# A fixed instruction order from a table, shared gate and up weights, and earlier closing waits in a fused attention and ReGLU kernel

## The chip, the core and the metric

The kernel runs on one core of a Trainium2 chip. The core has five engines that run side by side, each through its own list of instructions in order: PE (TensorE, matmuls, with PEld for its weight loads), ACT (ScalarE), DVE (VectorE), POOL (GpSimd) and SP (SyncE, which here only issues DMA transfers). They meet only through semaphores: an instruction can wait for a semaphore to reach a value, and can raise one when it is done. The metric is the time of one execution in microseconds (us) of device time, lower being better, as the median over runs.

## What is computed

The inputs are `x` of 2048 rows and 512 columns in bfloat16, and weights. The result is the input plus attention plus a gated feed-forward network, both on the same normalised input:

```python
xn  = layernorm(x)                                  # per row, eps 1e-5
qkv = xn @ wqkv                                     # 512 -> 3 * 512, 32 heads of 16
p   = softmax(q @ k.T / 4)                          # 32 heads, 2048 x 2048 scores each
att = (p @ v) @ wo
gate, up = xn @ W_gate, xn @ W_up                   # 512 -> 1792
ffn = (gate * (gate > 0) * up) @ W_down
out = x + att + ffn
```

The 32 x 2048 x 2048 = 134 million exponentials of the softmax are the peculiar part: heads are only 16 wide, so there is little matmul work for each exponential.

## The kernel before

**Tiles.** The 2048 query rows are cut into four blocks (`c4`), the 32 heads into four groups of eight (`gg`) and each group into its even and odd heads (`ee`): 32 blocks of four heads by 512 queries. Within a block the kernel goes through 16 tiles of 128 keys (`kt`). Scores stand in PSUM with keys on the partitions and 512 queries along the row, one head to a bank.

**Two ways to an exponential.** For most key tiles two *units* are made, each with two heads: two score matmul groups fill two PSUM banks, and one ACT instruction (line 1419) takes the exponential of 128 x 1024 values into a buffer `ring` of 16 places. There are 720 units; two pairs of banks are used in turn, so the scores of unit u wait until the exp of unit u-2 has read its banks. For the other key tiles, 152 in all and called *quads* (function `quad`), the exponential is approximated without ACT: DVE turns each head's scores into 16-bit integers that are the bit patterns of a power of two (`d1`, line 1372, 608 of them), and two shifted copies of these patterns are made, on POOL (line 1388, in two pieces each) or on DVE (line 1392). PE sums all three patterns.

**Matmuls.** Nearly all matmuls are of one form, issued by a helper at line 122: 64 x 32 weights with 512 moving columns. Four of them side by side make a *group*, and a group uses the lower or the upper half of the array's rows; groups on the two halves run at the same time. The weights of a group are loaded by four separate instructions (lines 1352 for scores, 1324 for values, 846 for the rest), and these are left out where the half still holds the same weights. Behind each unit and quad come groups that multiply the exponentials by the values (`pv_stream`) and add up in PSUM; a column of ones beside the values gives the sums of the softmax.

**The rest of the work** is laid between the units: projections of q, k and v (`proj_q`, `proj_k`, `proj_v`), the feed-forward network (`glu` makes 128 of the 1792 hidden columns for one block of 512 rows; `out_rows` multiplies by `W_down` and `wo` and stores the result), and the division by the sums (`normalise`), which goes through transfers of the sums to DRAM and back. A projected q is spread over `qT` by eight transfers of 16 KB. `glu` streams its gate and up weights from DRAM for two neighbouring hidden tiles at once, in two transfers of 128 KB each, into one of two buffers; it does so anew for every block of rows, which makes 56 transfers for each of the two. Four banks of PSUM are shared by all this, by the quads' scores and by the sums of `pv_stream`.

**The order.** All operations are first recorded in a graph (`Graph.op`) with an assumed duration, a priority, and what they read and write. `Graph.run` then places them one after the other: each time it takes the operation that could start first by the assumed durations, among those close together the one with the better priority, and gives it a buffer (`slot_for`, `ready`, `pick_pe`). What it leaves is a fixed list for each engine. `Graph.emit` works out which semaphore waits are needed, and `play` writes the instructions. On PE a load for the other half may be put ahead of a waiting group. The lists of the chip are thus static; an engine that waits holds up all that stands behind it in its own list.

**The end.** After the last unit `normalise_last` brings in the last block on a shorter path: a copy on ACT (line 1190), sums and transposes on DVE, eight more groups on PE, three additions on DVE and one copy on ACT, and four stores (line 1221). Each transfer belongs to a stream, and each stream has a semaphore; there are 102. At the very end SP waits for all of them (line 550):

```python
            if e == "SP":
                for s, v in fin:
                    eng.wait_ge(s, v)
```

## Time and profile before

| what | value |
|---|---|
| time, median of three runs | 695.08 us (691.43, 695.08, 696.24) |
| span of the profiled execution, the only time given of it | 696.8 us |
| PE busy | 678.8 us, 97% |
| PEld busy | 385.5 us, 55% |
| ACT busy | 671.8 us, 96% |
| DVE busy | 603.4 us, 87% |
| POOL busy | 504.2 us, 72% |
| DMA | 40.65 MB, mean 58 GB/s |

The page of the profile gives, for each engine, the busy time and its share, and for groups of equal instructions their count, their busy time together, the mean duration of one in ns, and the idle time of the engine just before them with what ended it. A group's busy time is shorter than count times mean where instructions overlap, as exps and matmuls do. "Issue" stands for time in which an engine waited for nothing that the profile shows. The chain is followed back from the last instruction, each time to what released it. Ends of matmuls are modelled, so that a busy PE is not PE at its peak. The mean clock granted to PE was 0.999 of full speed.

### The profile page before, as it was taken

What the parts mean: (1) busy time and instruction counts of PE and PEld (TensorE: products, weight loads), DVE (VectorE), ACT (ScalarE), POOL (GpSimd) and SP (SyncE); (2) the same over time, 40 slices, a digit from 0 to 9 for tenths busy, and PEclk for the clock granted to TensorE, in tenths of its full rate; (3) what the DMA queues carried; (4) which work ended last, traced back from release to release, by engine and by line L of the source; (5) the groups of instructions that cost most, each with busy time, mean ns of one, the idle gap of its engine ahead of it and who ended that gap; (6) DMA issues with size and microseconds to landing.
All of it is one profiled execution on the core that took longest, in us unless ns stands there. A gap on an engine that the chain in (4) does not pass through costs nothing.

```text
span 696.8 us, 46210 instructions
## 1 busy us (share of the span) xinstructions
PE 678.8 (97%) x22229; PEld 385.5 (55%) x20884; DVE 603.4 (87%) x1009; ACT 671.8 (96%) x733; POOL 504.2 (72%) x511
## 2 busy tenths in 40 slices
PE   8999999999999999999999999999999999999996
PEld 4556565555654656455655455654655575655663
DVE  9958899999899688888999887899999788899875
ACT  6999999999999999999999999999999999999994
POOL 3323759767689786868979787787778886786871
PEclk9999999999999999999999999999999999999999
DMA  7330312153201121211211121122210121221001
GB/s 212 71 65 6 92 46 63 46 140 96 63 27 40 41 80 55 52 47 56 68 35 33 41 78 49 49 62 58 58 54 25 48 72 50 62 58 40 27 17 48
DMA packets 65736, 40.65 MB, mean 58 GB/s; under 512 B 19912, under 2 KB 61576, under 8 KB 65544
## 3 DMA queue, kind: packets, MB, share of 16 engines
q1 hardware_dynamic: 65544, 37.69, 19.8%
q8 instruction: 169, 2.77, 1.7%
q14 instruction: 23, 0.19, 0.1%
HBM read 31.06 MB, written 2.35 MB: 48 GB/s over the span
## 4 chain that ended last, share of the span: by engine, by line
PE 62%; ACT 33%; DVE 2%; issue 1%; SPq 0%; DMA 0%; DVEq 0%
PE ps L122 61%; ACT ring L1419 32%; DVE qd L1372 1%; PE ps L950 1%; SPq L1288 0%; DVE xn_sb L775 0%; DVE v_aug L911 0%; DMA x_sb<-oT 0%; PE ps L800 0%; ACT qT L993 0%; PE ps L1434 0%; PE ps L968 0%; ACT xnT L808 0%; PE ps L1175 0%; DVEq L552 0%
## 5 line engine op out<-in xcount | busy, mean ns | idle before, releaser
L1419 ACT ACTIVATE ring<-ps 128x1024 bf16<-128x1024 f32 x720 | 665.5, 1102 | 8.5 <-PE ps L122 7.3
L1388 POOL TENSOR_TENSOR qd<-qd,ints 128x512 int32<-128x512 int32 x450 | 454.7, 1042 | 148.8 <-DVE qd L1392 58.7
L122 PE MATMUL ps<-qT,kT 64*32 64x512 bf16 x8192 | 463.5, 375 | 4.1 <-issue 0.9
L1372 DVE TENSOR_SCALAR qd<-ps 128x512 int16<-128x512 f32 x608 | 395.6, 684 | 56.5 <-PE ps L122 51.5
L122 PE MATMUL ps<-qd,v_aug 64*32 64x512 bf16 x3648 | 294.1, 375 | 1.3 <-issue 1.2
L122 PE MATMUL ps<-ring,v_aug 64*32 64x512 bf16 x2880 | 249.9, 375 | 0.5
L1352 PEld LDWEIGHTS <-kT 64*32 64x32 bf16 x7972 | 171.8, 92 | 123.8 <-issue 35.6
L1324 PEld LDWEIGHTS <-v_aug 64*32 64x32 bf16 x5400 | 131.8, 92 | 73.7 <-issue 18.6
L122 PE MATMUL ps<-xnT,wus 64*32 64x512 bf16 x1792 | 138.3, 375 | 1.1 <-issue 1.1
L122 PE MATMUL ps<-xnT,wgs 64*32 64x512 bf16 x1792 | 136.8, 375 | 0.6 <-issue 0.5
L1392 DVE TENSOR_SCALAR qd<-qd 128x2048 int16<-128x2048 int16 x79 | 62.8, 803 | 0.5
L846 PEld LDWEIGHTS <-wgs 64*32 64x32 bf16 x1792 | 44.1, 92 | 26.0 <-issue 5.8
L122 PE MATMUL ps<-Wd,hT 64*32 64x512 bf16 x768 | 56.8, 375 | 1.3 <-DVE qd L1372 0.5
L846 PEld LDWEIGHTS <-hT 64*32 64x32 bf16 x1792 | 44.2, 92 | 23.9 <-issue 4.9
L846 PEld LDWEIGHTS <-wus 64*32 64x32 bf16 x1792 | 44.1, 92 | 24.0 <-issue 5.5
L1057 DVE COPY up_sb<-ps 128x512 f32<-128x512 f32 x56 | 38.2, 683 | 4.6 <-PE ps L122 4.4
L122 PE MATMUL ps<-Wv,hT 64*32 64x512 bf16 x512 | 41.4, 375 | 0.8 <-issue 0.7
L1061 DVE SCALAR_TENSOR_TENSOR hT<-ps,up_sb 128x512 bf16<-128x512 f32 x56 | 38.2, 681 | 4.3 <-PE ps L122 4.0
L122 PE MATMUL ps<-Wk,hT 64*32 64x512 bf16 x512 | 40.5, 375 | 0.0
L122 PE MATMUL ps<-Wo_p,x_sb 64*32 64x512 bf16 x480 | 37.8, 375 | 0.0
L122 PE MATMUL ps<-xnT,Wq 64*32 64x512 bf16 x480 | 36.7, 375 | 0.2 <-issue 0.2
L122 PE MATMUL ps<-xnT,Wk 64*32 64x512 bf16 x480 | 34.2, 375 | 0.2 <-DVE xnT L816 0.2
(72 smaller groups left out, 267.4 us busy)
## 6 DMA issues: line engine op xcount, KB each, us to landing
rb<-rec_scr SPq DMA_DIRECT2D x31, 256.0 KB
wus<-in_B_W_up_dram SPq DMA_DIRECT2D x56, 128.0 KB, 3.1
wgs<-in_B_W_gate_dram SPq DMA_DIRECT2D x56, 128.0 KB, 2.8
xr_sb<-in_A_x_dram SPq DMA_DIRECT2D x16, 128.0 KB, 3.1
out_dram<-xn_sb SPq DMA_DIRECT2D x16, 128.0 KB, 1.8
qT<-qf SPq DMA_DIRECT2D x120, 16.0 KB, 2.8
x_sb<-in_A_x_dram SPq DMA_DIRECT2D x8, 128.0 KB, 2.6
x_sb<-oT SPq DMA_DIRECT2D x60, 16.0 KB, 2.6
```

Source lines behind the costliest of these rows:

```text
L122: return e.add_instruction(mybir.InstMatmult(name=e.bass.get_next_instruction_name(), engine=mybir.EngineType.PE, ins=[e.lower_ap(x), e.lo ...
L846: e.ldweights(w()[rows, 32 * j:32 * j + 32], tile_position=(rows.start, 32 * j))
L950: ins = e.matmul(ps[:, BANK[0], :], Wo_l[:, 0, 0:128], zeros, start=True, stop=True)
L1057: G.op("DVE", 603, lambda e: e.tensor_copy(up_sb[:, tup.slot, :], bank_of(tu)), reads=[tu], writes=[tup], prio=-590)
L1061: G.op("DVE", 603, lambda e: e.scalar_tensor_tensor(out=hT[:, th.slot, :], in0=bank_of(tg), scalar=0.0, in1=up_sb[:, tup.slot, :], op0=ALU ...
L1324: e.ldweights(vs(j), tile_position=(64 * half, 32 * j))
L1352: e.ldweights(ks(m), tile_position=(64 * half, 32 * m))
L1372: G.op("DVE", 601, lambda e, j=j, tx=tx: e.tensor_scalar(qd[:, tq.slot, 512 * j:512 * j + 512], ps[:, BANK[tx.slot], :], IBIAS[3], 0.0, op ...
L1388: G.op("POOL", POOL_NS / POOL_PIECES + 60, lambda e, x=x, n=n, c=slice(i * m, i * m + m): e.tensor_tensor(x().bitcast(I32)[:, c], raw().bi ...
L1392: G.op("DVE", 600, lambda e, n=n, x=x: e.tensor_scalar(x(), raw(), float(SHIFTS[n + 1]), None, op0=ALU.add), reads=[ti, tq], writes=[t], p ...
L1419: exp_ops[u] = G.op("ACT", 904, lambda e, tr=tr, k0=k0: e.activation(ring[:, tr.slot, :, :], ps[:, 4 * k0:4 * k0 + 2, :], ACTF.Exp, scale= ...
```

## The change

The change has four parts.

1. **The order is read from a table.** `Graph.run` no longer places operations by durations and priorities. A packed string, `PLAN`, holds the sequence of all 8245 operations (twelve filler matmuls for PE among them) and the place that each buffer takes; `run` unpacks it and appends the operations to the engines' lists in that sequence. The waits that keep buffers and banks apart are worked out as before from the sequence. New is a wait in front of a transfer: on each engine that reads what the previous transfer of the same stream brought, the first reader must be through.
2. **Which copies of quads POOL makes** is now written out in `QUAD_AT`, one row for each block and one character for each key tile: a dot for two units, a digit for a quad, whose two bits say which of its two shifted copies are POOL's. There are still 152 quads on the same key tiles, and 225 copies on POOL.
3. **Gate and up weights are loaded once for two blocks of rows** for some of the hidden tiles: six of the 14 in each of three pairs of neighbouring blocks. In the list of jobs the tile of the later block stands right behind that of the earlier.
4. **The closing waits** of all streams but those of the last four stores stand before the first of these stores on SP.

```diff
+LAST_STORES = 4
...
+QUAD_AT = (
+    "................",
+    ".0....3.....2...",
+    ".3...3...2...3..",
+    "2...3..3..0..3..",
+    "2...3..3..2..3..",
...
+    "2..3..3.0..0....",
+)
...
+PLAN_OPS = 8245
+PLAN = (
...
     def run(self):
-        ops = self.ops
...
+        ops, n = self.ops, len(self.ops)
+        plain = zlib.decompress(base64.b85decode(PLAN))
+        m = PLAN_OPS
+        self.queue = {e: [] for e in self.ENGS}
+        at, places = -1, iter(plain[2 * m:])
+        placed, bank, port, users, ahead = set(), {}, {"DVE": None, "POOL": None}, {}, {}
...
+        for i in range(m):
+            at += plain[i] * 256 + plain[m + i] - 65536 * (plain[i] > 127)
+            o = ops[at] if at < n else self.blank(at)
...
+                t.slot = next(places)
...
+            if o.eng == "SP":
+                for e in self.ENGS:
+                    us = [u for u in users.get(ahead.get(o.stream), ()) if u.eng == e and u is not o and o not in u.deps]
+                    if us:
+                        u = min((u for u in us if u in placed), key=lambda u: u.seq)
+                        if e != "SP":
+                            o.deps[u] = True
+                ahead[o.stream] = o
...
+            o.seq = len(self.queue[o.eng])
+            self.queue[o.eng].append(o)
+            placed.add(o)
...
+                if e == "SP" and i == len(self.queue[e]) - LAST_STORES:
+                    late = {id(q.sem[0]) for q in self.queue[e][i:]}
+                    for s, v in fin:
+                        if id(s) not in late:
+                            eng.wait_ge(s, v)
                 wait(o.waits)
                 ins = o.fn(eng)
...
             if e == "SP":
                 for s, v in fin:
-                    eng.wait_ge(s, v)
+                    if id(s) in late:
+                        eng.wait_ge(s, v)
...
-            if ft % 2 == 0:
+            if ft % 2 == 0 and (c4 == 0 or ft not in shared[c4 - 1]):
...
+        shared = [set(range(8, 14)), set(range(2, 8)), set(range(8, 14)), set()]
...
+            for ft in range(FT):
+                if c4 and ft in shared[c4 - 1]:
+                    continue
+                seq.append(ffn[ft])
+                if ft in shared[c4]:
+                    seq.append((0, GN, lambda s, c4=c4, ft=ft: glu(c4 + 1, ft, s), W_LEAD + 2))
...
+            mask = int(QUAD_AT[blocks.index(key[:3])][key[3]])
             for n, (t, x) in enumerate(((ta, xa), (tb, xb))):
-                share, off = ((POOL1_SHARE, P1_OFF), (POOL_SHARE, 0.0))[n] if nq[0] <= len(kinds) - LASTD else (0.0, 0.0)
-                if int(nq[0] * share + off) > int((nq[0] - 1) * share + off):
+                if mask >> n & 1:
```

## The prediction

> **What bounds the kernel now.** First the page of the profile: span, busy time, the queues, the chain that ended last, and the row of the exps.

> ```profile
> span 696.8 us, 46210 instructions
> PE 678.8 (97%) x22229; PEld 385.5 (55%) x20884; DVE 603.4 (87%) x1009; ACT 671.8 (96%) x733; POOL 504.2 (72%) x511
> q8 instruction: 169, 2.77, 1.7%
> PE 62%; ACT 33%; DVE 2%; issue 1%; SPq 0%; DMA 0%; DVEq 0%
> L1419 ACT ACTIVATE ring<-ps 128x1024 bf16<-128x1024 f32 x720 | 665.5, 1102 | 8.5 <-PE ps L122 7.3
> ```

> PE and ACT are both near full and the chain alternates between them. Two more views say who sets the pace: the row of the exps' line, with first and last start, and one piece of ACT's timeline in which nothing interrupts it.

> ```profile
> L1419 ACT ACTIVATE ring<-ps x720: 1017/1094/1312, 11.4 to 684.2; 128x1024 bf16<-128x1024 f32 x180
> 479.27 66.12 ACT L1419 ACTIVATE ring<-ps 128x1024 bf16<-128x1024 f32 x72 [0.55 <-PE ps L122]
> ```

> Undisturbed, ACT starts an exp every 66.12/72 = 0.918 us. From 11.4 to 684.2 there are 719 steps, 672.8/719 = 0.936 us each. At 0.918 they would take 660.1 us: 12.7 us are lost. Then stretches of 50 us (columns: length, then busy time and count of PE, PEld, DVE, ACT, POOL, then clock and DMA):

> ```profile
> 100.00:150.00 50.00, 49.89 (x1696) 28.78 (x1580) 47.21 (x77) 50.00 (x56) 37.72 (x38) 1.00 0.29 80
> 250.00:300.00 50.00, 48.85 (x1672) 26.98 (x1524) 42.67 (x68) 48.60 (x53) 40.17 (x40) 1.00 0.22 58
> 500.00:550.00 50.00, 49.11 (x1488) 24.73 (x1364) 44.72 (x75) 50.00 (x56) 42.04 (x42) 1.00 0.13 36
> 550.00:600.00 50.00, 49.39 (x1748) 32.43 (x1649) 41.26 (x64) 49.48 (x54) 38.49 (x39) 1.00 0.21 61
> 670.00:680.00 10.00, 10.00 (x376) 6.17 (x336) 6.00 (x9) 10.00 (x12) 7.95 (x8) 1.00 0.04 7
> ```

> The best stretches have 56 exps, at most 50/55 = 0.909 us each; by that 719 steps take 653.6 us and 19.2 us are lost. I take 16. The worst has 53. The array itself has room: 376 matmuls in 10 us are 47 groups of four on each half, 0.213 us a group, and 22,112 such matmuls need 2764 x 0.213 = 589 us. So what delays the exps is not matmul time. A piece of the chain (start, length, what), and then two rows of PE's timeline at its second stop, show what:

> ```profile
> 406.33 11.57 PE ps L122 x380
> 417.90 0.66 issue
> 418.57 11.65 PE ps L122 x394
> 430.21 0.14 issue
> 430.35 7.70 PE ps L122 x253
> 438.05 0.37 issue
> ```

> ```profile
> 417.49 0.10 PEld L846 LDWEIGHTS <-hT 64*32 64x32 bf16 x3
> ...
> 418.56 0.09 PEld L846 LDWEIGHTS <-hT 64*32 64x32 bf16 x1 [0.98 <-issue]
> ```

> ```profile
> 585.00:588.75 3.75, 3.75 (x130) 2.59 (x128) 3.31 (x6) 3.64 (x5) 2.45 (x3) 1.00 0.20 53
> 588.75:592.49 3.74, 3.74 (x137) 1.95 (x124) 3.41 (x7) 3.74 (x5) 3.74 (x4) 1.00 0.10 23
> ```

> 258 and 261 instructions in 3.75 us: that is the fastest the delivery goes, 256/3.75 = 68.3 per us, or 62.1 per exp of 0.909 us. The kernel needs 43,113/720 = 59.9 on average. It runs 4% under its limit for instructions; denser places make ACT wait.

> **The change part by part.** Its arithmetic stays: 720 exps, 608 `d1`, 450 POOL pieces, all 22,112 matmuls. Counted in the instruction order of both programs:

> ```profile
> L1352 PEld LDWEIGHTS <-kT 64*32 64x32 bf16 x7972 | 171.8, 92 | 123.8 <-issue 35.6
> L1324 PEld LDWEIGHTS <-v_aug 64*32 64x32 bf16 x5400 | 131.8, 92 | 73.7 <-issue 18.6
> wus<-in_B_W_up_dram SPq DMA_DIRECT2D x56, 128.0 KB, 3.1
> wgs<-in_B_W_gate_dram SPq DMA_DIRECT2D x56, 128.0 KB, 2.8
> qT<-qf SPq DMA_DIRECT2D x120, 16.0 KB, 2.8
> ```

> 1. *Fewer weight loads on PE.* With the new order two neighbouring groups of a half share weights more often: 7972 becomes 7732, 5400 becomes 4800. 840 instructions go; 42,273 remain, 58.7 per exp. Their own time lay under matmuls; what counts is delivery. Over runs of four exps (about one block) 38% of the runs of before need more than 62.1 per exp, 20% of after; the excess, added up and divided by 68.3 per us, is 11.8 us against 4.8. Over runs of twelve it is 5.9 against 2.0. So 3.9 to 7.0 us go if every block came at that rate. The stop of 0.66 us is longer than the rate explains, so some blocks come later, and there 2% more work in a block (0.08 us of 4) helps as well. I take 6.5, near the upper of the two for that reason; ends 0 and 11. [...]
> 2. *Smoother order.* Between two exps ACT's 0.909 us hold 0.909/0.213 = 4.3 groups a half. Pairs of neighbouring exps with 9 or more groups on a half between them fall from 227 to 158. Of the 16 us lost I put 10 on delivery and 6 on such bunching; a quarter of 6, 1.5 us, goes. Ends: 0 and 5.
> 3. *Gate and up loads shared.* 112 transfers of 128 KB become 76. They were no wait of PE or ACT, so the transfers themselves are worth nothing; one that is late would stop a group. They free the path of q8's blocks, within the ends of 1.
> 4. *Buffers taken again sooner.* PE's waits for DVE that stand ten groups or fewer behind the matmul they stem from rise from 139 to 187. Everything behind such a wait, scores too, stands in PE's queue.

> ```profile
> PE ps L122 <- DVE qd L1372: 0.5, 1, 0.5
> DVE qd L1372 <- PE ps L122: 51.5, 97, 1.7
> L1372 DVE TENSOR_SCALAR qd<-ps 128x512 int16<-128x512 f32 x608 | 395.6, 684 | 56.5 <-PE ps L122 51.5
> ```

> In before such waits emptied PE for 0.5 us in all; if each met one more DVE operation it would cost 0.684 us. 48 more of them: 0 to 33 us; nearest to the first row, 0.02 each, +1.0 us.

> 5. *SP.* A transfer now also waits for one reader of the previous transfer on its stream, and what stands behind it on SP waits too. SP's instructions with a wait fall from 208 to 162, and the nearest reader of a `qT` copy stands 53 groups behind its source instead of 57, some 53 x 0.107 = 5.7 us, against 2.8 us to land. I put it at nothing; if that cover fails, fifteen projections times half a microsecond, +7.5.
> 6. *The end.*

> ```profile
> 683.60 0.39 PE L122 MATMUL ps<-qT,kT 64*32 64x512 bf16 x8
> 685.96 0.66 ACT L1190 ACTIVATE up_sb<-ps 128x256 f32<-128x256 f32 x2 [0.57 <-PE ps L122]
> L1221 SPq DMA_DIRECT2D out_dram<-xn_sb x4: 350/442/511, 691.1 to 692.8; - x4
> DMA to landing us min/median/max: 1.8/1.9/1.9
> L550 SPq EVENT_SEMAPHORE  x51: 17/28/28, 693.3 to 696.3; - x51
> SPq L1221 <- DVE xn_sb L1216: 11.0, 2, 10.8
> ```

> The last store is issued at 692.8 and landed at 694.7; 51 closing waits, 0.06 us apart, run to 696.3. With only the four stores' waits behind them the program is through at about 694.75: -1.6 us. The others, 3 us, now stand before the first store, in SP's 10.8 us of idleness. Against it, behind the last scores stand 50 groups instead of 39, of them 11 on the lower half ahead of its last `pv`: 11 x 0.213 + 0.375 (a matmul) = 2.72 us to the copy of L1190, 2.36 before (683.60 to 685.96): +0.35.

> Sum: -6.5 - 1.5 + 1.0 - 1.6 + 0.35 = -8.25 us against the span of 696.8, which is all the page gives of that execution, so 688.5. The span stands 1.7 us over the median of the runs, 695.08; taken off the median: **687**.

> **The rivals.**

> *Delivery is hidden.* The stops of PE are swallowed by the lead that scores have over their exps, or the blocks of the new order come late as often as those of the old, and then fewer loads buy nothing. Then 2, 4 and 6 remain: -1.75, 693.3. For it: issue is only 1% of the chain, 7 us. Against it: the torn group, and 53 exps in the stretch 250 to 300. [...]

> *Recycling decides, and the kernel is slower.* The 48 closer waits of 4 each find DVE still busy with one operation more. Without item 4 the change gains 9.25 us; slower by 1% needs 9.25 + 7.0 = 16.2 us, 0.34 us a wait, half a DVE operation. At 0.45: 695.1 + 21.6 - 9.25 = 707. For it: DVE is 87% busy, `d1` waits for PE in turn. Against it: the row of 0.5 us.

> *All slack.* If every exp has its scores in time, the whole 16 us go: 695.1 - 16 - 1.25 = 678. For it: the mean density of 58.7 is 5% under the limit. Against it: a fifth of the runs stay above it.

> **How the numbers follow.** One per cent, 7 us, is about what a measurement of this kernel can tell from no change (its three runs span 4.8). Chances: forecast (682 to 690.5) 0.46, all slack (under 682) 0.20, hidden (690.5 to 698) 0.22, recycling (over 698) 0.12. Faster by over 1% is under 688.1: all slack and three quarters and more of the forecast, 0.56. Slower is over 702.0: 0.10. Within: 0.34. The range leaves out a tenth at each end: 678 to 699.

> **What would show it.** Right: about 165 transfers on q8; exps in stretches of 50 us at 55 or 56 everywhere; the issue pieces of the chain fewer and shorter; the step between exps near 0.92 us; the program through within 2.2 us of the last store's issue. Wrong: the same count of issue pieces at 53 exps; PE waiting for DVE by microseconds; POOL or `qT` copies as releasers of PE in the chain.

## The result and the profile after

The kernel after takes 691.9 us (median of 20 runs, 690.9 to 695.0), the kernel before on the same chip 696.5 us (20 runs, 691.4 to 699.4). The ratio is **0.9937, 95% interval 0.9922 to 0.9951**: 4.6 us or 0.6% faster, where 687.0 and 1.2% were forecast.

The page of the kernel after, the same rows as were shown of before:

```profile
span 689.1 us, 45379 instructions
...
PE 680.3 (99%) x22232; PEld 355.1 (52%) x20044; DVE 600.3 (87%) x1009; ACT 669.8 (97%) x733; POOL 503.1 (73%) x511
...
q8 instruction: 165, 2.70, 1.6%
...
PE 88%; DVE 5%; ACT 4%; SPq 1%; DMA 1%; issue 0%; POOL 0%; DVEq 0%
...
L1376 ACT ACTIVATE ring<-ps 128x1024 bf16<-128x1024 f32 x720 | 663.5, 1100 | 3.8 <-PE ps L251 2.7
```

q8 moves the 165 blocks that were forecast, and ACT's idleness before exps falls from 8.5 to 3.8 us. Three more rows of after: the exps' line and the last stores with first and last start, and the closing waits that still stand behind the stores:

```profile
L1376 ACT ACTIVATE ring<-ps x720: 1017/1098/1277, 11.2 to 677.4; 128x1024 bf16<-128x1024 f32 x180
```

```profile
L1180 SPq DMA_DIRECT2D out_dram<-xn_sb x4: 348/436/576, 685.2 to 686.8; - x4
```

```profile
L513 SPq EVENT_SEMAPHORE  x2: 17/22/28, 688.2 to 688.7; - x2
```

Read against the rows of before, the two spans split into four pieces:

| piece | before | after | difference |
|---|---|---|---|
| start to first exp | 11.4 | 11.2 | -0.2 |
| first to last exp | 672.8 | 666.2 | -6.6 |
| last exp to last store's issue | 8.6 | 9.4 | +0.8 |
| last store's issue to the end | 4.0 | 2.3 | -1.7 |

That is -7.7 us between the two profiled executions, against -8.25 forecast, while the medians are 4.6 us apart. The nearness of -7.7 to the forecast is luck. The profiled execution of after took 690.9 us, the fastest of its 20 and 1.0 us below their median; that of before took, estimated from its span, some 698.6 us, 2.1 us above its own. Together these make up the 3.1 us between 7.7 and 4.6. So the first question is not where a gain went, but how much of it was ever there.

Stretches of 50 us of after (columns as in the prediction):

```profile
200.00:250.00 50.00, 49.54 (x1630) 25.32 (x1440) 42.61 (x71) 49.23 (x54) 41.17 (x41) 1.00 0.09 25
250.00:300.00 50.00, 50.00 (x1720) 26.58 (x1528) 44.52 (x72) 50.00 (x55) 42.02 (x42) 1.00 0.24 68
...
500.00:550.00 50.00, 49.40 (x1564) 23.31 (x1366) 45.94 (x76) 49.92 (x56) 40.65 (x40) 1.00 0.11 29
550.00:600.00 50.00, 50.00 (x1756) 27.11 (x1596) 41.38 (x67) 49.89 (x56) 37.78 (x38) 1.00 0.20 60
```

The stretch from 250 has 55 exps in place of 53, that from 550 has 56 in place of 54; the good ones are no better than before. The waits of PE that no semaphore explains, first in before, then in after (total us, times, longest):

```profile
PE ps L122 <- issue: 5.0, 12, 0.8
```

```profile
PE ps L251 <- issue: 0.2, 1, 0.2
```

### The profile page after: what moved, and what is told of

Same layout as the page of the kernel before. It is cut to its first block, busy times and chain, and to the rows that moved or that the text cites. A ratio compares the mean times of both kernels' runs of the same rounds, so it can differ in the third digit from the quotient of the medians.

```text
span 689.1 us, 45379 instructions
## 1 busy us (share of the span) xinstructions
PE 680.3 (99%) x22232; PEld 355.1 (52%) x20044; DVE 600.3 (87%) x1009; ACT 669.8 (97%) x733; POOL 503.1 (73%) x511
## 4 chain that ended last, share of the span: by engine, by line
PE 88%; DVE 5%; ACT 4%; SPq 1%; DMA 1%; issue 0%; POOL 0%; DVEq 0%
PE ps L251 88%; ACT ring L1376 4%; DVE qd L1331 1%; DVE stats L725 1%; SPq L857 1%; DVE xn_sb L738 1%; DMA x_sb<-oT 1%; SPq L1247 0%; DMA x_sb<-in_A_x_dram 0%; DVE up_sb L1014 0%; DVE qd L1350 0%; DVE xnT L779 0%; DVE v_aug L874 0%; POOL rstd L720 0%; DVE mv L726 0%
## 5 line engine op out<-in xcount | busy, mean ns | idle before, releaser
L251 PE MATMUL ps<-qT,kT 64*32 64x512 bf16 x8192 | 451.6, 374 | 1.2 <-ACT ring L1376 0.3
L251 PE MATMUL ps<-qd,v_aug 64*32 64x512 bf16 x3648 | 266.4, 375 | 0.4
L251 PE MATMUL ps<-ring,v_aug 64*32 64x512 bf16 x2880 | 241.9, 375 | 0.1
L1311 PEld LDWEIGHTS <-kT 64*32 64x32 bf16 x7732 | 158.9, 92 | 126.4 <-issue 34.2
L1283 PEld LDWEIGHTS <-v_aug 64*32 64x32 bf16 x4800 | 114.2, 91 | 79.0 <-issue 25.3
L251 PE MATMUL ps<-xnT,wgs 64*32 64x512 bf16 x1792 | 139.5, 375 | 0.1
L1350 DVE TENSOR_SCALAR qd<-qd 128x2048 int16<-128x2048 int16 x79 | 53.8, 693 | 2.6 <-PE ps L251 2.4
L809 PEld LDWEIGHTS <-hT 64*32 64x32 bf16 x1792 | 40.8, 92 | 26.1 <-issue 3.2
L251 PE MATMUL ps<-Wk,hT 64*32 64x512 bf16 x512 | 43.9, 375 | 0.0
L251 PE MATMUL ps<-Wv,hT 64*32 64x512 bf16 x512 | 43.9, 375 | 0.0
## 6 DMA issues: line engine op xcount, KB each, us to landing
wus<-in_B_W_up_dram SPq DMA_DIRECT2D x38, 128.0 KB, 2.7
wgs<-in_B_W_gate_dram SPq DMA_DIRECT2D x38, 128.0 KB, 3.1
xr_sb<-in_A_x_dram SPq DMA_DIRECT2D x16, 128.0 KB, 3.1
out_dram<-xn_sb SPq DMA_DIRECT2D x16, 128.0 KB, 2.3
x_sb<-in_A_x_dram SPq DMA_DIRECT2D x8, 128.0 KB, 2.8
```

The source lines that it names most:

```text
L251: return e.add_instruction(mybir.InstMatmult(name=e.bass.get_next_instruction_name(), engine=mybir.EngineType.PE, ins=[e.lower_ap(x), e.lo ...
L809: e.ldweights(w()[rows, 32 * j:32 * j + 32], tile_position=(rows.start, 32 * j))
L1283: e.ldweights(vs(j), tile_position=(64 * half, 32 * j))
L1311: e.ldweights(ks(m), tile_position=(64 * half, 32 * m))
L1350: G.op("DVE", 600, lambda e, n=n, x=x: e.tensor_scalar(x(), raw(), float(SHIFTS[n + 1]), None, op0=ALU.add), reads=[ti, tq], writes=[t], p ...
```

## A measure for the stops, and four chips

Two sums, worked out from each trace, stand in what follows. *Stops*: PE's instructions are numbered in order of start, and the gaps over 60 ns that fall on one fixed place modulo 256 are added up (the first six and last blocks left out). In before that place gives 22.2 us; the median over the 255 other places is 2.0, so some 20 us are stops at the ends of blocks. *Loss*: the time from first to last exp less 719 steps of 0.904 us, the commonest step. *Block* is the mean duration of a transfer on q8.

| chip | kernel | stops, us | loss, us | block, us | time, us | ratio to before, same chip |
|---|---|---|---|---|---|---|
| first | before | 22.2 | 22.8 | 1.15 | 696.5 | 1 |
| first | after | 5.4 | 16.2 | 1.07 | 691.9 | 0.9937 |
| A | before, closing moved | 14.1 | 17.4 | 1.07 | 689.9 | 0.9971 (0.9952 to 0.9990) |
| A | after, loads put back | 9.2 | 18.0 | 1.09 | 691.6 | 0.9996 (0.9981 to 1.0011) |
| B | after | 3.0 | 15.1 | 1.05 | 690.9 | 0.9982 (0.9967 to 0.9998) |
| C | before, closing moved | 16.4 | 20.1 | 1.12 | 693.8 | 0.9972 (0.9952 to 0.9993) |
| C | after | 7.1 | 18.6 | 1.15 | 693.2 | 0.9961 (0.9943 to 0.9980) |
| D | before, twice | 11.1, 12.1 | 15.9, 16.8 | 1.08, 1.07 | 691.6 | 1 |
| D | after | 3.0 | 15.1 | 1.07 | 690.5 | 0.9990 (0.9977 to 1.0004) |

The kernel before took 691.8 us on A, 692.4 on B and 695.7 on C; each group of runs below ran on one of these chips. The record doesn't name the first chip, so it may be one of A to D. The change is worth most where the kernel before is slowest.

The traces also show what ends a stop. Between any two neighbouring block ends of PE, in every profile of the table and from the sixth block on, there lies exactly one transfer on q8, and PE never passed a block's end less than about 1.2 us after that transfer was through. In before all 24 stops of more than 0.3 us at this place ended 1.2 to 1.6 us behind it; so did all 9 and all 13 in the two profiles of before on D. Read so, these stops are waits for a block, of which one came between any two ends. From PE's passing a block's end to the end of the next transfer it takes 2.29 us on average in before on the first chip, 2.09 and 2.07 on D, 1.98 in after on the first chip. Over the five profiles of the order of before the stops grow with this time, from 2.07 to 2.29 us, but for the two on D, which stand 0.02 us apart. The shortest time from one block's end to the next was 3.47 us in before: the 3.75 us of the prediction are no fixed limit.

## Was the first profile typical?

The kernel before unchanged, two more profiles, on chip D.

> The kernel before, unchanged, for a second profile of it. Theory 1, the block stops of PE vary from execution to execution and the first profile showed a bad one: stops at every 256th instruction of 8 to 18 us in all, and a span of 689 to 694. Theory 2, they belong to the kernel: 20 us or more and a span of 695 or more.

> The kernel before, unchanged, for a third profile. Theory 1: its sum of block stops differs from that of the run before it in this call by 2 us or more, and its span with it, although chip and program are the same. Theory 2: both agree within 1 us.

The first of the two (span, exps, PE's unexplained waits, and the same weight load that the prediction showed torn):

```profile
span 690.0 us, 46210 instructions
```

```profile
L1419 ACT ACTIVATE ring<-ps x720: 1017/1128/1312, 11.6 to 677.5; 128x1024 bf16<-128x1024 f32 x180
```

```profile
PE ps L122 <- issue: 2.2, 4, 1.2
```

```profile
413.16 0.10 PEld L846 LDWEIGHTS <-hT 64*32 64x32 bf16 x3
413.69 0.09 PEld L846 LDWEIGHTS <-hT 64*32 64x32 bf16 x1 [0.43 <-issue]
```

And the second:

```profile
span 690.6 us, 46210 instructions
```

```profile
413.31 0.33 PEld L846 LDWEIGHTS <-hT 64*32 64x32 bf16 x4
```

It is the same instruction by number in all three: torn for 0.98 us in the profile that the prediction had, for 0.43 and, by the starts of PE's instructions, for 0.20 in these. Stops are 11.1 and 12.1 us, spans 690.0 and 690.6. Theory 1 of the first expectation came: 22 us of stops are not a fixed property of the kernel. The two on one chip differ by 1.0 us in stops and 0.6 in span, so the second expectation goes to its theory 2. Whether the first profile stood high for its chip or for that one execution, no run separates.

## The parts of the change

**Closing waits.** Moved alone in the kernel before, on A and on C, and put back alone in the kernel after, on C beside the kernel after unchanged:

```diff
+                if e == "SP" and i == len(self.queue[e]) - LAST_STORES:
+                    late = {id(q.sem[0]) for q in self.queue[e][i:]}
+                    for s, v in fin:
+                        if id(s) not in late:
+                            eng.wait_ge(s, v)
...
-                    eng.wait_ge(s, v)
+                    if id(s) in late:
+                        eng.wait_ge(s, v)
```

```diff
+EARLY_CLOSING = False
...
-                        if id(s) not in late:
+                        if id(s) not in late and EARLY_CLOSING:
...
-                    if id(s) in late:
+                    if id(s) in late or not EARLY_CLOSING:
```

> The kernel before with the closing waits of all streams but the last four stores' moved ahead of these stores, nothing else. Both theories: 1.6 us faster than before, the program through within 2.2 us of the last store's issue.

> The kernel before with the closing waits moved in front of the last four stores, nothing else. Theory 1, this is most of what the change is worth where the blocks of PE come well: 1.6 to 2.0 us faster than the kernel before, and within 1 us of the kernel after unchanged. Theory 2, the order and the sharing are worth some us on every chip: the kernel after is faster than this one by 2 us or more.

> The kernel after with its closing waits put back behind the last store (order, sharing and quads as after). Theory 1: the closing waits are worth their 1.7 us in this order too, so this kernel is slower than the kernel after by 1.5 to 2.0 us and stands within 1 us of the kernel before on a chip where that is at 692. Theory 2, order and sharing earn their own 2 us or more on every chip: faster than the kernel before by 2 us or more.

> The kernel after, unchanged, to stand beside the other three of this call on the same chip. Ratio to the kernel before 0.994 if the first chip was typical, 0.998 if the kernel before is again at 692.

Ratios to before: 0.9971 on A and 0.9972 on C, 2.0 and 1.9 us; in after, 0.9993 against 0.9961 on C, 2.2 us by the ratios, 1.9 by the medians (695.1 and 693.2). The rows of the two ends: span, last stores, then closing waits of the kernel after with late waits; and span and last stores of after beside it:

```profile
span 693.0 us, 45376 instructions
```

```profile
L1181 SPq DMA_DIRECT2D out_dram<-xn_sb x4: 332/364/443, 687.0 to 688.6; - x4
```

```profile
L514 SPq EVENT_SEMAPHORE  x51: 17/28/28, 689.1 to 692.5; - x51
```

```profile
span 691.8 us, 45376 instructions
```

```profile
L1180 SPq DMA_DIRECT2D out_dram<-xn_sb x4: 347/428/525, 687.9 to 689.5; - x4
```

4.4 us from the last store's issue to the end against 2.3. This part is worth its 2 us in both orders, as the three expectations on it had it; after unchanged beside it, 0.9961, lies between its two figures. On C the kernel before with it alone, 0.9972, is as fast as the whole change, 0.9961, within the intervals; after unchanged did not run on A. Seen from the other side, all the rest of the change, without the moved waits, stands at 0.9993 (0.9978 to 1.0008) on C: 0.5 us, which can't be told from nothing.

**Sharing alone**, with the order still made by the planner of before; 36 transfers of 128 KB fewer.

```diff
-            if ft % 2 == 0:
+            if ft % 2 == 0 and (c4 == 0 or ft not in shared[c4 - 1]):
...
-                k = (c4 * FT + ft) // 2
+                k = len(ws_made)
+                ws_made.append(ft)
...
+            for ft in range(FT):
+                if c4 and ft in shared[c4 - 1]:
+                    continue
+                seq.append(ffn[ft])
+                if ft in shared[c4]:
+                    seq.append((0, GN, lambda s, c4=c4, ft=ft: glu(c4 + 1, ft, s), W_LEAD + 2))
```

> The kernel before with the sharing of gate and up weights alone, the order still made by its own planner (weight loads on PE stay as many: 20,808 for 20,764; 36 transfers fewer). Theory 1 with blocks delayed by transfers: 1 to 2 us faster. If transfers do not matter: within 1 us of before, or worse by what the planner makes of the other sequence.

1.0040 (1.0021 to 1.0058) on B, 2.8 us slower. Theory 1 missed. Stops are 7.5 us, but the loss is 17.4 and the end after the last exp 13.9 us long (12.5 in before on D): the planner lays another list, and that probably costs more than the blocks gain; before itself was not profiled on B. The order and the sharing cannot be valued apart from each other this way.

**Traffic.** In the kernel before, gate and up transfers from the third pair on bring 32 of the 128 rows, so that the rest of these weights is left from earlier ones.

```diff
-                            dst[:, tw.slot, dt:dt + 2, :], src[128 * dt:128 * dt + 256, 128 * ft:128 * ft + 256].rearrange("(dt p) f -> p dt f", p=128)), 128,
+                            dst[0:(128 if k < 2 else 32), tw.slot, dt:dt + 2, :], src[128 * dt:128 * dt + 256, 128 * ft:128 * ft + 256].rearrange("(dt p) f -> p dt f", p=128)[0:(128 if k < 2 else 32)]), 128,
```

> The kernel before, same order and same transfers, but from the third pair of hidden tiles on each gate or up transfer brings 32 of its 128 rows, a quarter of the bytes (the other rows keep older weights, so the output is another one). If transfers delay the blocks of PE's program: the long stops become rarer and the kernel 2 to 4 us faster. If not: within 1 us.

```profile
wus<-in_B_W_up_dram SPq DMA_DIRECT2D x52, 32.0 KB, 2.6
```

0.9961 (0.9944 to 0.9979) on B, 2.7 us faster by that ratio with not one instruction less on PE; stops 8.9 us, loss 14.9. No row had shown PE or ACT waiting for these transfers. That they delay PE's blocks can be read within the traces: in the five profiles of the order of before, blocks during whose fetch gate or up transfers were under way landed 0.18 to 0.27 us later after PE's passing the last block's end than the others did (2.43 against 2.19 us in the first profile), and 0.10 us later with the cut transfers. That the whole 2.7 us come this way is not shown, as before was not profiled on B.

**Loads.** In the kernels before and after, three of the four weight loads of each gate, up, down and output group are left out (4368 instructions; these products then use weights of another group), and in the kernel after 888 loads of all kinds that it saves are put back.

```diff
-                for j in range(4):
+                for j in range(1 if light else 4):
```

```diff
-                o.load, o.wsrc = False, ()
+                again += 1
+                if again * 210 // 517 == (again - 1) * 210 // 517:
+                    o.load, o.wsrc = False, ()
```

> The kernel before, same order, with three of the four weight loads left out in every group of the gate, up, down and output matmuls (4368 of 43,113 PE instructions; those columns use the weights that happen to stand there, so the output is another one). Theory 1, delivery of PE's program: about 152 blocks instead of 169, hardly any stop at a block's end, 6 to 10 us faster than before, some 688 us. Rival, the stops are covered by the scores' lead and the order alone matters: within 1 us of before.

> The kernel after with the same loads left out. Theory 1: after has next to no stops at blocks' ends left, so at most 1.5 us faster than after. If delivery still costs it something that its trace hides: 4 us or more. If e1 comes out as fast as this one, the change's whole gain was delivery; if this one is faster by some us, the rest is the order's own.

> The kernel after, same order, with 888 of the left-out weight loads put back (loads of weights that stand there already), so that PE has about as many instructions as before. Theory 1: 4 to 7 us slower than after, some 697, with stops at blocks' ends again. Rival: within 1 us of after.

On A: 0.9960 (0.9947 to 0.9973) for before, 2.8 us faster for 4368 loads, between theory 1 (6 to 10) and the rival; stops are down to 5.7 and the loss to 14.5. After with fewer loads is at 0.9961 (0.9945 to 0.9978), with a loss of 14.7; it has the closing waits moved, which the other has not, and yet is no faster. After unchanged did not run on A, so how far this run and the next lie from it, as their expectations put it, was not measured; the 697 us named for the next one didn't come. After with loads put back is at 0.9996: 691.6 us, against 689.9 for before with the closing waits moved, which has the same loads within 48, the transfers that after saves, and the old order. So **without its saved loads the new order looks 1.7 us worse than the old one**; the two intervals, 0.9981 to 1.0011 and 0.9952 to 0.9990, still overlap, and the loads were put back at other places than before had them. Part of that is the end after the last exp, 11.5 us against 10.8; most of the rest would have to lie between the exps, where the profiles show 18.0 against 17.4 us lost, with stops of 9.2 against 14.1.

## What is left between the exps

In their best runs both orders still lose 14.5 to 15.1 us: before 14.5 with fewer loads and 14.9 with less traffic, after 15.1 unchanged on B and D and 14.7 with fewer loads. Three cuts in the kernel after ask what that is, each beside after on its chip.

DVE's shifted copies at a quarter of their width from unit 60 on (the rest of the patterns stays old), on B beside after unchanged:

```diff
-                G.op("DVE", 600, lambda e, n=n, x=x: e.tensor_scalar(x(), raw(), float(SHIFTS[n + 1]), None, op0=ALU.add),
+                G.op("DVE", 600, lambda e, n=n, x=x, c=slice(0, 2048 if u < 60 else 512): e.tensor_scalar(x()[:, c], raw()[:, c], float(SHIFTS[n + 1]), None, op0=ALU.add),
```

> The kernel after with the shifted copies that DVE makes cut to a quarter of their width from unit 60 on (columns beyond keep older patterns, so the output is another one); some 30 us of DVE time go, instructions and order stay. If what still delays exps in after is PE waiting for DVE to free banks: 3 us or more faster than after. If it is the bunching of groups on PE: within 1 us of after.

> The kernel after, unchanged, beside the kernel before on the chip of the other runs of this call. On the chip of the first experiments the kernel before stood at 691.8 us, 4.7 us less than where the change was measured. If what the change removes is the stops at blocks' ends, and these cost before less on this chip, the gain is smaller here: 2 to 3 us, after at 689 to 690. If the gain is the order's own it is 4 to 5 us again, 687.

```profile
L1350 DVE TENSOR_SCALAR qd<-qd 128x512 int16<-128x512 int16 (+1 forms) x79 | 23.0, 302 | 3.1 <-PE ps L251 2.8
```

0.9976 (0.9961 to 0.9992) against 0.9982, loss 15.1 in both, with 31 us less of these copies: DVE's load is not it. After unchanged gained 1.2 us on B, less than either of the two figures expected of it.

Gate, up, down and output matmuls at half their columns, on C:

```diff
-                        ins = matmul_loaded(e, d[c, :], ww[rows, c], xx[rows], start, stop, (rows.start, 32 * j))
+                        ins = matmul_loaded(e, d[c, 0:256] if light else d[c, :], ww[rows, c], xx[rows][:, 0:256] if light else xx[rows], start, stop, (rows.start, 32 * j))
```

> The kernel after with the moving columns of the gate, up, down and output matmuls halved from 512 to 256 (that half of their results is not computed; same instructions, same order, weight loads, transfers and waits). In the kernel after some 14 to 15 us of the steps between exps are lost over 0.904 us each also where PE hardly stops at the ends of its blocks. Theory 1, what is left is bunching: the order puts more group time between two exps than a step holds, and shorter groups thin these places: at least 5 us faster than the kernel after on the same chip, loss between exps under 10 us. Theory 2, what is left is not array time but instructions or the hand-over between PE and ACT: within 1.5 us of it, loss of 13 us or more.

```profile
L251 PE MATMUL ps<-xnT,wgs 64*32 64x256 bf16 x1792 | 92.5, 268 | 0.4 <-issue 0.2
```

A gate matmul falls from 375 to 268 ns, and the kernel, over four runs, to 0.9924 (0.9899 to 0.9950) from 0.9961: 2.6 us, loss 15.7 from 18.6. That lies between the two theories, nearer to the second. Array time is a small part, by these 2.6 us.

The DVE operation that frees the banks of a quad's scores at half its width from unit 110 on, on D:

```diff
-                G.op("DVE", 601, lambda e, j=j, tx=tx: e.tensor_scalar(
-                    qd[:, tq.slot, 512 * j:512 * j + 512], ps[:, BANK[tx.slot], :], IBIAS[3], 0.0, op0=ALU.add, op1=ALU.max),
+                G.op("DVE", 601, lambda e, j=j, tx=tx, m=512 if u < 110 else 256: e.tensor_scalar(
+                    qd[:, tq.slot, 512 * j:512 * j + m], ps[:, BANK[tx.slot], 0:m], IBIAS[3], 0.0, op0=ALU.add, op1=ALU.max),
```

> The kernel after, in which the DVE operation that turns a head's scores of a quad into integers takes only the first 256 of 512 columns, for quads from unit 110 on (the other half is not computed). Everything else, order and waits too, is as in after. Theory 1, the largest of what is left between exps is PE waiting for DVE to free a bank of PSUM, with the next scores behind it: at least 4 us faster than the kernel after on the same chip, and the time that the two halves of PE wait for DVE ahead of scores of quads at least halved. Theory 2, what is left are places where the order puts five or more groups on a half between two exps, and the hand-over of the exp's own banks: within 2 us of the kernel after.

> The kernel after, unchanged, to stand beside the others of this call. Time 690.5 to 693.5; block stops of 3 to 8 us in its profile; ratio to the kernel before between 0.994 and 0.998.

```profile
L1331 DVE TENSOR_SCALAR qd<-ps x608: 359/425/694, 24.4 to 674.5; 128x256 int16<-128x256 f32 x139, 128x512 int16<-128x512 f32 x13
```

0.9971 (0.9955 to 0.9987) against 0.9990: 1.3 us. The halves of PE wait 12.1 us in all for DVE ahead of a quad's scores in place of 24.8, so the wait was halved as theory 1 had it, but the loss stayed at 15.0 and the gain under 2 us: theory 2. Of 12.7 us of such waits 1.3 us came back as time; that the lead of the scores over their exps covers the rest was not shown. After beside it came at the time and the stops that were expected, but with a ratio of 0.9990, above the 0.998 that bounded it.

In the kernel after the late exps are nearly always the same ones: over five profiles of its order (four of after unchanged, one with the late closing waits), 69 of the 719 steps are late by more than 60 ns in the median, 12.0 us together, and many by the same amount to a few ns (exp 222 by 304 to 310 ns in all five). One is this, in the profile of after:

```profile
227.03 0.38 PE L251 MATMUL ps<-Wd,hT 64*32 64x512 bf16 x4 [0.46 <-DMA x_sb<-oT]
...
227.67 1.02 ACT L1376 ACTIVATE ring<-ps 128x1024 bf16<-128x1024 f32 x1 [0.34 <-PE ps L251]
```

The row puts the wait down to a transfer of attention results. But ahead of this group PE has ten semaphore waits in a row, the row's transfer among them, and takes 0.106 us for each:

```profile
L483 PEldq EVENT_SEMAPHORE  x10: 51/51/54, 225.9 to 226.9; - x10
```

In the profile of after on D the last of these transfers was in at 227.42, the tenth wait came only at 227.76, and the exp is 0.63 us late all the same, as against 0.55 here. So it is the string of waits, about 1.06 us with scores behind, that delays this exp; the order of before has it too, and there the same exp is 0.68 to 0.77 us late. Other late exps have nine groups on a half between two exps. No single cause was found whose removal takes more than 2.6 us; what the rest is stays open.

## Why the prediction was right and wrong

**What failed.** The step that failed is term 1 of the sum, -6.5 us for fewer weight loads, together with the way in which it was carried to the median. Its mechanism was seen, its size was that of the stops in one long execution. Terms 1, 2 and 4 with the longer tail were to give -6.65 us. Measured on C, where the closing waits alone were put back, all of this gives 0.5 us; on the first chip some 2.6 us remain of the 4.6 when the closing waits are taken at 2 us, an estimate from A and C. Why so little of the stops' time turns into gain stays open in part: other waits stand in its place (in the steps counted under 2 below, on D 8.7 us in after for 8.0 to 8.8 in before), and the lead of the scores may cover some of it, which no run shows by itself.

**From one execution to the median: wrong.** "Taken off the median" the sum gave 687. Where both are known, a run's time stands 1.7 to 1.8 us above its span (after: 690.9 and 689.1). The execution behind the profile of before thus took some 698.6 us, 2 us above its kernel's median over 20 runs and 3.5 above the 695.08 from which the sum was taken. By its own base the forecast was 688.5 + 1.8 = 690.3 us, and that execution of after took 690.9, but it was the fastest of 20. The prediction said that the page gives only the span, and then took what this long execution could lose from the time of a shorter one.

**1, fewer loads, -6.5: the mechanism right, the size that of one profile.** Between the two profiles items 1, 2 and 4 were to give -7.0 us, and the exps show -6.6; stops fell from 22.2 to 5.4. But on D, where before has 11 to 12 us of stops, the whole change gives 0.9990. There the stops go all the same (to 3.0, near the 2 us of any place, 8 to 9 us less) and only 0.8 to 1.7 us of loss go with them. The size came from a limit of 256 instructions in 3.75 us, taken as fixed, while the time from one block's end to the next block's landing was 2.29 us in that profile and 2.07 to 2.09 on D. Little of the stops' time thus came back between the exps on D; on the first chip more did, 6.6 us of loss for 16.8 us of stops. The rival *delivery is hidden*, at -1.75 us, is nearest to what D shows; the first chip lies between it and the forecast.

**2, smoother order, -1.5: not shown.** Steps late by 20 ns or more with five groups or more on a half and no long stop lose 5.2 us in before and 4.2 in after, 1.0 less; but how much this is hangs on how groups are put to steps, and when those are counted that start between the two exps it is 2.3 to 2.9 us in three profiles of before and 2.4 to 2.6 in two of after. Steps with a stop over 0.1 us on a half lose 8.0 to 8.8 us in before on D and 8.7 in after there, though its block stops are gone: other waits stand there. With the loads put back, the order looks 1.7 us behind the old one.

**3, shared loads, nothing by themselves: right in kind.** No row shows PE or ACT waiting for them, and blocks landed 0.18 to 0.27 us later under them; the run with little traffic gained 2.7 us on B.

**4, buffers sooner, +1.0: not contradicted.** Halves of PE wait for DVE ahead of a quad's scores at 186 places for 25.3 us, in before at 129 for 21.6, by sums over the traces; taking half of the wait away was worth 1.3 us. The closer waits alone were not measured, and no row gives the 0.02 us that the term takes for each. *Recycling decides* didn't happen.

**5, SP, nothing: nothing against it.** The fifteen late copies of the other end didn't appear; the wait put down to a transfer above is a string of ten waits on PE, which before has too.

**6, the end: -1.6 was -1.7 in the profiles, 1.9 to 2.2 in the comparisons. +0.35 for the longer tail was +0.8.** The tail was counted as groups alone, to the first copy. That copy starts 2.3 us after the last exp's start where it was 1.7:

```profile
679.72 0.66 ACT L1149 ACTIVATE up_sb<-ps 128x256 f32<-128x256 f32 x2 [1.27 <-PE ps L251]
```

The rest comes between this copy and the stores.

On the signs listed: 165 transfers and fewer and shorter issue pieces came as said (53 of 2.8 us in all for 62 of 7.5); the end came 2.3 us behind the last store's issue, just over the 2.2. The step came out at 666.2/719 = 0.927 us, not quite near 0.92, and one stretch still had 54 exps. *All slack* fell: even with 4368 loads fewer 14.5 us of loss remain. The 16 us of loss that it rests on are 22.8 us in that profile when a step is taken at 0.904 us.

## What to carry to other kernels

Before a gain is sized on stalls in one profile, compare that execution's own time with the median, and where stalls come from delivery, look at a second profile: here the same torn group lost 0.98, 0.43 and 0.20 us. Fewer instructions per exp can be worth having (4368 loads less gave 2.8 us on A), but stops taken away are not time won: on D 8 to 9 us of stops went, and 0.8 to 1.7 us of loss. The cheap, certain part of a large change can be most of it: 48 waits moved into idle time were worth 2 us, on two chips in the old order and on one of them in the new.

## What was not expected of the hardware

In the kernel before PE stopped at a fixed place of every 256 instructions (22.2 us there against 2.0 in the median of the other places, first chip), and how long varied from profile to profile of the same program: 22.2 on one chip, then 11.1 and 12.1 us in all on another, with a mean block transfer of 1.15, 1.08 and 1.07 us. In the program of before and its variant with moved waits, five profiles, stops grow with the loss (from 11.1 and 15.9 us to 22.2 and 22.8), but the mean block transfer alone doesn't order them. All stops of more than 0.3 us at that place, 24, 9 and 13 in the three profiles of before, ended 1.2 to 1.6 us behind the end of a block's transfer. DMA traffic that no row shows PE waiting for cost time in the one run that took it away, 2.7 us on B for three quarters of most gate and up transfers, and in the profiles of the order of before blocks landed 0.18 to 0.27 us later under it. In the string of ten, a wait for a semaphore took PE 0.106 us also where there was nothing left to wait for.
